# One kernel for attention and two expert layers: other forms of the routing comparisons beside layer two's products, ScalarE as the gate of four weight transfers, and another instruction order

## The chip, the cores and the metric

The program runs on one core of a Trainium2 chip. The metric is the device time of one execution in microseconds (us); the median of three runs counts. In the profile PE is TensorE, DVE is VectorE, ACT is ScalarE, POOL is GpSimd and SP is the queue that issues most transfers.

## What is computed

Attention over 4 x 8 heads (768 positions, head size 64, a few global keys and a local window), then an expert layer with a gate (layer one), then a second expert layer with a limit per expert (layer two). Of the reference, layer two matters here:

```python
cap = N // E                                   # 3072 // 8 = 384
logits = x @ w_gate
order = np.argsort(-logits.flatten())
for idx in order:
    tok, e = idx // E, idx % E
    if assigned[tok] >= 0 or counts[e] >= cap: continue
    assigned[tok] = e; counts[e] += 1
for e in range(E):
    h = np.maximum(x[assigned == e] @ w1[e], 0.0)
    out[assigned == e] = h @ w2[e]
```

## The kernel before, in words

**Layer two's products.** Each of the eight experts gets exactly 384 tokens. An expert's work is a *unit*: eight blocks `f`, each with 12 products into `ph` (384 columns; the inputs are split in a high and a low float32r part, so `xh,wh`, `xl,wh` and `xh,wl`) and 9 products into three banks `py` (512 columns). That is 168 products for a unit and 1344 for the layer.

**Routing (`phase`, `slots`, L1738 and L1859).** The greedy assignment is done in eight phases. In a phase each free token holds its best logit (`m`) and its expert (`oh`, one-hot). The phase finds the highest threshold at which some expert has more than its remaining places, fills that expert and takes it out. The threshold is found by seven comparisons (`BITS`: six of five bits with 32 thresholds each, and a last one of two bits with 4). One comparison is: VectorE compares all tokens with the thresholds (`gm`), TensorE counts per expert (`pr<-oh,gm`), VectorE picks the next threshold. A count comes in two forms:

- *direct*: 24 small products of 32 rows by 8 columns, one for each group of 128 tokens, then VectorE's flags `fl`, one more product with the table `wt`, and a VectorE maximum;
- *grouped* (`CG = 4`): 6 products of four token groups each, of which only a quarter of the result is wanted, a copy `cs` on VectorE, and a product that adds the quarters up. From phase 2 on (`LEAN`) the copy masks and one product with `sel` is enough (*lean*); otherwise there are four with `sels`. VectorE then takes the maximum, a 32 x 32 transpose and a weighted sum, with no flag product.

In the kernel before, the first 13 comparisons of all (`DIRECT`) are direct: phase 0 whole and six of phase 1. A phase's last comparison, of 4 thresholds, is always followed by the flag product, and from phase 1 on it is grouped in a narrow form (16 columns, four products with `identh`). After the comparisons a phase adds a visit with two products `pr<-c,tri`, a visit with `pr<-part,ones`, and two in `slots` (`pt<-ttb`, `pt<-tb_rhs,mp`), whose result is the expert's list of tokens, `ids`. GpSimd then gathers the expert's rows (`xg<-x2d,ids`, three transfers), TensorE transposes them (`x_turn`), ScalarE writes `xh` and VectorE `xl`.

**What sets the order.** Phase 0 runs beside the last second-layer products of layer one (`py`, 417 to 450 us), phase 1 begins before the first unit and goes on beside it, and phase p runs beside unit p - 1. All instructions are recorded through a planner: `Clock` holds a time for each engine with a cost for every operation (`cost`), and before each product `hook` (L1240) asks every open *stream* (routing, row lists, transpositions) whether its next step would be ready (`when`, L1223); if so, the step is recorded there, so TensorE's queue gets it ahead of the product. TensorE works in that order and waits when a step's operand is late. While nothing else is to be done `warm` fills TensorE with `ph<-ones,tri`.

**Weights.** A chunk of 512 KB comes into one of four buffers `wr`; ScalarE writes its high part `wh`, GpSimd (in four pieces) or VectorE the low part `wl`. Around the start of layer two, four transfers are held back by a 1 x 1 write into their buffer (`do_load`, `gate`), which the transfer has to follow: by VectorE before the change. The loop at the kernel's end (L2023) lets them go one by one as the first unit's blocks are turned.

Nearly all instructions carry L132, the recording helper's line, so rows are told apart by their tiles.

Of the kernel before, what the change touches and what calls it, by code (L numbers as in the profile page):

```python
# [19 lines left out]
class Clock:  # L20
# [4 lines left out]
    def __init__(self):  # L25
        self.at = dict.fromkeys(("pe", "dve", "act", "pool", "sp", "dma"), 0.0)
        self.seen, self.slots, self.count, self.log = {}, {}, {}, {}
        self.on = False
        self.late, self.fine = 0, False
# [46 lines left out]
    def cost(self, eng, op, outs, ins, extra):  # L76
        n = max([1] + [a.free_size() for a in outs[:1] + ins])
        if eng == "pe":
# [6 lines left out]
            return max(0.027, n * (2 if op == "transpose" else 4 if d.endswith("float32") else 1) / 2400.0)  # L85
# [85 lines left out]
def tile_attn_moe_moe(ctx: ExitStack, tc: tile.TileContext, q, k, v, n_global, n_local,  # L171
# [277 lines left out]
    class Weights:  # L449
# [58 lines left out]
        def do_load(self, i):  # L508
# [4 lines left out]
            if self.gate:  # L513
                nc.vector.memset(t[0:1, 0:1], 0.0)
# [46 lines left out]
    LATE = 0.3  # L561
# [649 lines left out]
    class Stream:  # L1211
# [287 lines left out]
    tabs = [rt.tile([128, 32], I32, name="tabf")] + [rt.tile([128, n_], I32, name=f"tab{s_}") for s_, n_ in BITS[1:]]  # L1499
    wt_ = rt.tile([32, 128], BF, name="wt")  # L1500
# [33 lines left out]

    blocks = identh.rearrange("p (j n) -> p j n", n=32)
# [22 lines left out]
    def ww_rest():  # L1558
# [4 lines left out]
                + [rt_rows, rt_sel, rt_sels])  # L1563
# [167 lines left out]
    def phase(ph_):  # L1731
# [8 lines left out]
        for it, (s_, n_) in enumerate(() if last else BITS):  # L1740
            if it and any(s_.kind == 'x' for s_ in streams):
                yield "dve", ()
            gm_ = rt.tile([128, NT * 32], BF, name="gm")
            gm = gm_[:, :NT * n_].rearrange("p (t n) -> p t n", n=n_)
# [44 lines left out]
            if wide:  # L1789
                df = rt.tile([128, E], F32, name="df")  # L1790
                fr = rt.tile([128, 2, 32], F32, name="fr")
                dv.tensor_tensor_reduce(df, cnt[:, :E], rem, 1.0, -3.0e38, op0=OP.subtract, op1=OP.max,
                                        accum_out=v_[:, 0:1])
                dv.transpose(fr[:, 0], v_[:, 0:1].to_broadcast([128, 32]))
                dv.scalar_tensor_tensor(fr[:, 1], fr[:, 0], 0.0, wrow_p, op0=OP.is_ge, op1=OP.mult, accum_out=v_[:, 1:2])
# [14 lines left out]
            else:  # L1810
                dv.scalar_tensor_tensor(nx[:, 1, :nn], val.to_broadcast([128, nn]), s_, nx[:, 0, :nn],
                                        op0=OP.logical_shift_left, op1=OP.bitwise_xor)
# [3 lines left out]
        if last:  # L1816
            dv.scalar_tensor_tensor(fo[:, 0], rem, 1e8, first, op0=OP.is_lt, op1=OP.mult)
        else:
            dv.scalar_tensor_tensor(fo[:, 0], pn_, v_[:, 1:2], first, op0=OP.is_equal, op1=OP.mult)
        dv.tensor_reduce(fx[:, 0:1], fo[:, 0], axis=AX.X, op=OP.max)  # L1820
        wait_for(lambda: not [s_ for s_ in streams if s_.kind == "ids"])
        yield "dve", ()
        fe = rt.tile([128, 6, NT], F32, name="fe", bufs=2)
        if not last:
            ts_ = thr.bitcast(F32)
            sc, g1 = fe[:, 2:4], fe[:, 1]
# [16 lines left out]
        if last:  # L1843
            yield "dve", ()
            dv.tensor_scalar(fe_p, PEN, 0.0, None, op0=OP.is_ge)
            dv.scalar_tensor_tensor(fe[:, 4], AC, fx[:, 0:1], fe_p, op0=OP.is_equal, op1=OP.add)
# [12 lines left out]
        dv.tensor_tensor(fe[:, 4], fe_p, g1, op=OP.add)  # L1859
        start("ids", slots(ph_, fe, fx))  # L1860
        yield "dve", ()
        go = rt.tile([128, NT, E], BF, name="go")
        part = rt.tile([128, E], BF, name="part")
        dv.tensor_tensor(go, oh, bc_e(gt[:, 0]), op=OP.mult)
        dv.tensor_tensor(gt[:, 0], gt[:, 0], g1, op=OP.add)
        with nc.allow_low_precision(reason="whole numbers up to 24"):
# [199 lines left out]
```

## Time and profile before

| what | value |
|---|---|
| median of three runs (lowest to highest) | 775.62 us (775.53 to 776.88) |
| the profiled execution's own time | 777.47 us |
| its span, first to last instruction | 775.7 us |
| PE busy | 744.8 us, 96% |
| DVE, ACT, POOL busy | 526.1, 403.3, 468.2 us |
| layer two: first product to last | 464.57 to 770.40 us |
| before it, filler, routing and the first gather | 450.52 to 464.57 us |

The page's own second section shows PE at nine tenths or more in 20 of 40 slices and PEclk at nine tenths or more in all. A busy PE is not one at its peak: busy time counts a product from start to modelled end, and products overlap. So the rows below are read by the distance from one start to the next.

### The profile page before, as it was taken

How to read it: one execution, taken by the hardware profiler on the slowest of the kernel's cores; microseconds unless marked ns; L12 is line 12 of the kernel's file. 1: busy time of each engine (PE TensorE's matmuls, PEld its weight loads, DVE VectorE, ACT ScalarE, POOL GpSimd, SP SyncE). 2: the span in 40 equal slices, each digit the busy share in tenths (PEclk: the TensorE clock that was granted, in tenths of full speed). 3: DMA queues.
4: the chain of work that ended last, by engine and by line, in shares of the span. 5: the costliest groups of instructions: out<-in, count | busy, mean ns of one | idle time of the engine just before them, and what ended most of it. 6: DMA issues, size and time to landing. Idle time of an engine off the chain costs nothing.

```text
span 775.7 us, 17432 instructions
## 1 busy us (share of the span) xinstructions
PE 744.8 (96%) x5910; PEld 628.7 (81%) x5910; DVE 526.1 (68%) x1952; ACT 403.3 (52%) x936; POOL 468.2 (60%) x821
## 2 busy tenths in 40 slices
PE   7999999899889999999999999999999999999997
PEld 5887777677659999999888677878788878788986
DVE  5987988979556676777634586778787778752110
ACT  5887787887547655555652113434333434255221
POOL 4664456755214464555793636975768777689911
PEclk9999999999999999999999999999999999999999
DMA  8686988897716766777760035626262636366311
GB/s 192 167 213 167 248 232 200 222 231 199 236 27 213 265 198 195 252 234 224 210 220 33 19 91 191 209 91 222 77 204 84 230 108 206 125 195 185 121 41 41
DMA packets 145370, 132.23 MB, mean 170 GB/s; under 512 B 65427, under 2 KB 112787, under 8 KB 145280
## 3 DMA queue, kind: packets, MB, share of 16 engines
q1 hardware_dynamic: 136896, 111.19, 48.9%
q0 software_dynamic: 6784, 19.51, 7.4%
q8 instruction: 48, 0.79, 0.4%
q10 hardware_dynamic: 1600, 0.39, 0.2%
q14 instruction: 42, 0.34, 0.1%
HBM read 108.80 MB, written 22.79 MB: 170 GB/s over the span
## 4 chain that ended last, share of the span: by engine, by line
PE 44%; POOL 8%; issue 6%; DMA 5%; DVE 4%; ACT 3%; POOLq 0%; DVEq 0%; ACTq 0%; SPq 0%
PE py L132 19%; PE ph L132 19%; POOL wl L132 7%; DMA wr<-in_moe_w_dram 4%; PE pr L132 3%; PE pt L132 3%; ACT wh L132 2%; DVE wl L132 1%; POOL out_dram L132 1%; DMA xg<-x2d,ids 1%; DVE py L132 1%; ACT ya L132 0%; DVE h L132 0%; POOL xg L132 0%; DVE o L132 0%
## 5 line engine op out<-in xcount | busy, mean ns | idle before, releaser
L132 POOL TENSOR_TENSOR wl<-wr,wh 128x256 fp32r<-128x256 f32 x356 | 253.6, 745 | 62.0 <-ACT wh L132 61.3
L132 ACT ACTIVATE wh<-wr 128x1024 fp32r<-128x1024 f32 (+1 forms) x148 | 142.2, 985 | 42.8 <-DMA wr<-in_moe_w_dram 26.8
L132 PE MATMUL py<-wh,h 128*128 128x512 f32 (+1 forms) x448 | 155.9, 401 | 0.0
L132 ACT ACTIVATE h<-ph 128x208 fp32r<-128x208 f32 (+2 forms) x132 | 54.4, 415 | 180.7 <-PE ph L132 168.3
L132 POOL TENSOR_SCALAR pb<-pb,st 128x232 f32<-128x232 f32 (+1 forms) x192 | 83.4, 453 | 74.3 <-ACT pb L132 24.2
L132 ACT ACTIVATE pb<-sb,st 128x232 f32<-128x232 f32 (+1 forms) x192 | 113.8, 664 | 10.1 <-DVE st L132 9.8
L132 DVE SCALAR_TENSOR_TENSOR h<-ph,h 128x208 fp32r<-128x208 f32 (+1 forms) x128 | 58.8, 460 | 88.8 <-ACT h L132 88.7
L132 PE MATMUL ph<-xh,wh 128*128 128x208 f32 (+1 forms) x512 | 99.1, 310 | 1.4 <-DVE h L132 1.4
L132 PE MATMUL ph<-xh,wl 128*128 128x208 f32 (+1 forms) x512 | 100.0, 311 | 0.0
L132 PE MATMUL ph<-xl,wh 128*128 128x208 f32 (+1 forms) x512 | 99.0, 311 | 0.0
L132 PEld LDWEIGHTS py<-wh,h 128*128 128x128 f32 (+1 forms) x448 | 82.0, 185 | 14.1
L132 PE MATMUL py<-wl,h 128*128 128x512 f32 (+1 forms) x224 | 90.9, 406 | 0.0
L132 PEld LDWEIGHTS ph<-xh,wh 128*128 128x128 f32 x512 | 82.2, 190 | 6.8 <-DVE h L132 1.6
L132 PEld LDWEIGHTS ph<-xl,wh 128*128 128x128 f32 x512 | 78.9, 190 | 1.1 <-issue 1.0
L132 PEld LDWEIGHTS ph<-xh,wl 128*128 128x128 f32 x512 | 78.9, 190 | 0.5 <-issue 0.3
L132 DVE TENSOR_TENSOR wl<-wr,wh 128x1024 fp32r<-128x1024 f32 x47 | 61.0, 1304 | 15.3 <-ACT wh L132 15.2
L132 DVE CUSTOM_DVE_ANT_0 sb<-pS,bias 128x232 f32<-128x232 f32 (+1 forms) x192 | 61.4, 374 | 8.9 <-PE pS L132 7.6
L132 DVE COPY pts<-pP 116x512 f32<-116x512 f32 (+1 forms) x96 | 60.7, 672 | 7.6 <-PE pP L132 7.1
L132 POOL DMA_INDIRECT xg<-x2d,ids x24 | 23.8, 990 | 52.2 <-DVE ids L132 19.1
L132 PE MATMUL pS<-kt,qt 64*128 64x232 f32 (+1 forms) x384 | 50.7, 382 | 1.0 <-ACT pb L132 1.0
L132 PE MATMUL pP<-ident,pb 128*116 128x128 f32 (+1 forms) x384 | 51.3, 277 | 0.0
L132 PE MATMUL pO<-pts,vw 116*64 116x128 f32 x640 | 46.3, 281 | 4.0 <-DVE pts L132 3.2
(465 smaller groups left out, 1267.5 us busy)
## 6 DMA issues: line engine op xcount, KB each, us to landing
wr<-in_moe_w_dram SPq DMA_DIRECT2D x136, 512.0 KB
xd<-xs SPq DMA_DIRECT2D x32, 192.0 KB
x2d<-xs SPq DMA_DIRECT2D x32, 192.0 KB
kraw<-in_k_dram SPq DMA_DIRECT2D x30, 192.0 KB
qraw<-in_q_dram SPq DMA_DIRECT2D x30, 192.0 KB
vw<-in_v_dram SPq DMA_DIRECT2D x32, 160.0 KB
vw<-in_v_dram SPq DMA_DIRECT2D x32, 120.0 KB
xT<-in_moe_w_dram SPq DMA_DIRECT2D x1, 1536.0 KB
```

Source lines behind the costliest of these rows:

```text
L132: r = f(*a, **k)
```

## The change

The change leaves what is computed as it is. Direct counts are used only until layer two's first unit has begun (`unit_no < 0`), in place of the first 13. From phase 2 on the last comparison has 32 thresholds like the others (`lean_low`), with two tables of their own (`tab8`, `zero8`, made once by `rt_eights`; and `jrow`), and takes the lean grouped form without flag product. Also from phase 2 on, `part` is computed early (`above`), and its product stands in one visit with the two of `tri`. The gate's 1 x 1 writes are ScalarE's, and a gate opens when a block is turned (`len(xt)`), not when its low part is recorded. The planner's costs for layer two are raised: 0.016 us for each float32r product, 0.085 us for a long product behind a short one. `LATE` goes from 0.3 to 0, and two kinds of waiting (`gm`, `ids`) get rules of their own in `when`. Renumbered planes of `fe` are left out of the diff here.

```diff
@@ Clock.cost
-            return max(0.027, n * (2 if op == "transpose" else 4 if d.endswith("float32") else 1) / 2400.0)
+            t = (0.016 if self.fine and d.endswith('float32r') else 0) + max(0.027, n * (2 if op == "transpose" else 4 if d.endswith("float32") else 1) / 2400.0)
+            back, self.short = self.short and t > 0.1, t < 0.06
+            return t + (0.085 if back else 0)
@@ Weights.do_load
-                nc.vector.memset(t[0:1, 0:1], 0.0)
+                nc.scalar.activation(t[0:1, 0:1], pcol[0:1], AF.Copy)
-    LATE = 0.3
+    LATE = 0.0
@@ Stream.when
+            if eng == "gm":
+                return ck.at["dve"] - 0.1
+            if eng == "ids":
+                return 1e9 if [s_ for s_ in streams if s_.kind == "ids"] else ck.at["dve"] - T_SP
@@ phase
             if it and any(s_.kind == 'x' for s_ in streams):
-                yield "dve", ()
+                yield "gm", ()
+            low = it + 1 == len(BITS)
+            lean_low = low and ph_ >= LEAN
+            n_ = 32 if lean_low else n_
-            nn = BITS[it + 1][1] if it + 1 < len(BITS) else 1
+            nn = 1 if low else 32 if ph_ >= LEAN else BITS[it + 1][1]
-            tb_ = tabs[it + 1] if it + 1 < len(BITS) else zero
+            tb_ = zero8 if lean_low else zero if low else tab8 if ph_ >= LEAN and it + 2 == len(BITS) else tabs[it + 1]
-            low = it + 1 == len(BITS)
-            direct = ph_ * len(BITS) + it < DIRECT
-            wide = not direct and not low
+            direct = unit_no[0] < 0
+            wide = not direct and (not low or lean_low)
...
-                dv.tensor_tensor_reduce(df, cnt[:, :E], rem, 1.0, -3.0e38, op0=OP.subtract, op1=OP.max,
-                                        accum_out=v_[:, 0:1])
+                if lean_low:
+                    dv.tensor_tensor(df, cnt[:, :E], rem, op=OP.is_ge)
+                    dv.tensor_tensor_reduce(df, df, first, 1.0, 0.0, op0=OP.mult, op1=OP.max, accum_out=v_[:, 0:1])
+                else:
+                    dv.tensor_tensor_reduce(df, cnt[:, :E], rem, 1.0, -3.0e38, op0=OP.subtract, op1=OP.max,
+                                            accum_out=v_[:, 0:1])
...
-        wait_for(lambda: not [s_ for s_ in streams if s_.kind == "ids"])
-        yield "dve", ()
+        yield "ids", ()
...
+        both = ph_ > 1
+        if both:
+            above()
-        yield "pe", [c2]
+        yield "pe", [c2, part] if both else [c2]
         te(pp[:, 0, 0:1], tri2, c2[:, 0:1], start=True, stop=False)
         te(pp[:, 0, 0:1], tri, c2[:, 1:2], start=False, stop=True)
+        if both:
+            pq = pp[:, 1, :E]
+            te(pq, ones, part, start=True, stop=True)
...
@@ end of the kernel
-        wait_for(lambda: units2[0].tb == tb, True)
+        wait_for(lambda: len(units2[0].xt) >= tb, True)
```

How the order moves is shown at three places. The first is VectorE just before layer two's first product, in phase 1's first two comparisons (`xl` is the low part of one turned block; the `gm` of two pieces is one comparison's). Before:

```order
L132 TENSOR_TENSOR gm<-m,py_7060 128x512
L132 TENSOR_TENSOR gm<-m,py_7060 128x256
L132 TENSOR_TENSOR py_7060<-tab_4447,py_7060 128x32
L132 TENSOR_TENSOR xl<-pt,xh 128x4x128
L132 MEMSET wr 1x1
L132 TENSOR_TENSOR xl<-py_7748,xh 128x4x128
L132 MEMSET wr 1x1 x3
L132 TENSOR_TENSOR fl<-pr,rem 32x8
L132 TENSOR_TENSOR xl<-py_7784,xh 128x4x128
```

and now:

```order
L134 TENSOR_TENSOR fl<-pr,rem 32x8
L134 TENSOR_TENSOR xl<-pt,xh 128x4x128
L134 TENSOR_REDUCE v__7725<-pr 128x1
L134 TENSOR_SCALAR py_7064<-v__7725 128x1
L134 TENSOR_SCALAR vi<-v__7725 128x1
L134 TENSOR_TENSOR py_7064<-tab_4446,py_7064 128x32
L134 TENSOR_TENSOR py_7064<-py_7064,vi 128x32
L134 TENSOR_TENSOR xl<-py_7733,xh 128x4x128
L134 TENSOR_TENSOR gm<-m,py_7064 128x512
L134 TENSOR_TENSOR gm<-m,py_7064 128x256
L134 TENSOR_TENSOR py_7064<-tab_4447,py_7064 128x32
L134 TENSOR_TENSOR xl<-py_7763,xh 128x4x128
```

The low parts of the first and second block now stand ahead of the second comparison's `gm`, and the four 1 x 1 writes are gone.

The second is TensorE in phase 2, from the fourth comparison's product with `sel` to the start of the next count. Before:

```order
L132 LDWEIGHTS sel
L132 MATMUL pr<-cs,sel 128x32
L132 MATMUL py_7894<-wl,h_8414 128x512
L132 MATMUL py_7894<-wh,h_8414 128x512
L132 MATMUL ph<-xh,wh 128x384 x4
L132 MATMUL ph<-xl,wh 128x384 x4
L132 MATMUL ph<-xh,wl 128x384 x4
L132 LDWEIGHTS gm
L132 MATMUL pr<-oh,gm 128x32
```

and now:

```order
L134 MATMUL pr<-cs,sel 128x32
L134 MATMUL py_7899<-wh,h_8372 128x512
L134 MATMUL py_7899<-wl,h_8372 128x512
L134 MATMUL py_7899<-wh,h_8372 128x512
L134 MATMUL py_7900<-wh,h_8372 128x512
L134 MATMUL py_7900<-wl,h_8372 128x512
L134 MATMUL py_7900<-wh,h_8372 128x512
L134 MATMUL py_7901<-wh,h_8372 128x512
L134 MATMUL py_7901<-wl,h_8372 128x512
L134 MATMUL py_7901<-wh,h_8372 128x512
L134 MATMUL ph<-xh,wh 128x384
L134 LDWEIGHTS gm
```

Between the two stood two products of 512 columns and twelve of 384; now nine of 512 and one of 384 stand there.

The third is GpSimd, from one of the last gathers to the gather for the last unit (`out_dram` is an expert's result being written). Before:

```order
L132 DMA xg_10968<-x2d,ids 128x512
L132 DMA xg_10970<-x2d,ids 128x512
L132 DMA xg_10972<-x2d,ids 128x512
L132 TENSOR_TENSOR wl<-wr,wh 128x256 x32
L132 DMA xg_11259<-x2d,ids 128x512
L132 DMA xg_11261<-x2d,ids 128x512
L132 DMA xg_11263<-x2d,ids 128x512
L132 TENSOR_TENSOR wl<-wr,wh 128x256 x8
L132 MEMSET spacer 1x1
L132 DMA out_dram<-o_11253,ids 3072x512
```

and now:

```order
L134 TENSOR_TENSOR wl<-wr,wh 128x256 x8
L134 MEMSET spacer 1x1
L134 DMA out_dram<-o_10879,ids 3072x512
L134 TENSOR_TENSOR wl<-wr,wh 128x256 x8
L134 MEMSET spacer 1x1
L134 DMA out_dram<-o_10881,ids 3072x512
L134 TENSOR_TENSOR wl<-wr,wh 128x256 x4
L134 MEMSET spacer 1x1
L134 DMA out_dram<-o_10883,ids 3072x512
L134 TENSOR_TENSOR wl<-wr,wh 128x256 x12
L134 DMA xg_11207<-x2d,ids 128x512
L134 DMA xg_11209<-x2d,ids 128x512
```

The last unit's gather (the second one of the two) stood behind 32 pieces of `wl` in a row. Now there are 32 pieces between the two gathers as well, but three results are written among them.

## Rows read from the trace of the kernel before

**Rows 1.** Stages: start:end, length, busy (x) of PE, PEld, DVE, ACT, POOL, clock, DMA.
```profile
464.57:770.40 305.83, 304.02 (x1853) 256.12 (x1851) 187.66 (x761) 118.17 (x171) 215.21 (x312) 1.00 0.45 146
```

**Rows 2.** Groups by form, layer two, PE: direct counts, narrow last counts | busy, mean ns.
```profile
L132 PE MATMUL pr<-oh,gm 128*32 128x8 bf16 x96 | 3.0, 167 | 0.5 <-DVE gm L132 0.5
...
L132 PE MATMUL pr<-oh,gm 128*16 128x32 bf16 x36 | 1.8, 177 | 0.0
```

**Rows 3.** Timeline of PE, unbroken products: start, us, operation, xcount.
```profile
531.26 0.85 PE L132 MATMUL ph<-xl,wh 128*128 128x384 f32 x4
...
532.65 0.40 PE L132 MATMUL py<-wh,h 128*128 128x512 f32 x1
...
552.51 0.40 PE L132 MATMUL py<-wh,h 128*128 128x512 f32 x1
...
554.57 0.33 PE L132 MATMUL ph<-xh,wh 128*128 128x384 f32 x1
```

**Rows 4.** Timeline of PE, phase 1: one direct comparison.
```profile
466.38 0.51 PE L132 MATMUL ph<-xh,wl 128*128 128x384 f32 x2
466.82 0.76 PE L132 MATMUL pr<-oh,gm 128*32 128x8 bf16 x24
467.51 0.62 PE L132 MATMUL ph<-xh,wl 128*128 128x384 f32 x2
...
468.97 0.85 PE L132 MATMUL ph<-xl,wh 128*128 128x384 f32 x4
```

**Rows 5.** Timeline of PE, phase 2: one lean comparison, and the next count.
```profile
509.79 0.39 PE L132 MATMUL py<-wl,h 128*128 128x512 f32 x1
510.02 0.32 PE L132 MATMUL pr<-oh,gm 128*128 128x32 bf16 x6
...
510.75 0.19 PE L132 MATMUL pr<-cs,sel 128*128 128x32 f16 x1
...
511.11 0.39 PE L132 MATMUL py<-wh,h 128*128 128x512 f32 x1
...
513.43 0.32 PE L132 MATMUL pr<-oh,gm 128*128 128x32 bf16 x6
```

**Rows 6.** Timeline of PE, phase 2: first and last row around a last comparison.
```profile
518.79 0.62 PE L132 MATMUL py<-wh,h 128*128 128x512 f32 x2
...
521.51 0.86 PE L132 MATMUL ph<-xh,wh 128*128 128x384 f32 x4
```

**Rows 7.** Timeline of PE, phase 2: the visit with part.
```profile
526.88 0.18 PE L132 MATMUL pr<-part,ones 128*128 128x8 bf16 x1
...
527.52 0.86 PE L132 MATMUL ph<-xh,wl 128*128 128x384 f32 x4
```

**Rows 8.** Timeline of PE at layer two's start.
```profile
459.59 0.76 PE L132 MATMUL pr<-oh,gm 128*32 128x8 bf16 x24 [0.29 <-DVE gm L132]
...
463.23 0.66 PE L132 MATMUL py<-ident,xg 128*128 128x128 f32 x4
...
464.57 0.62 PE L132 MATMUL ph<-xh,wh 128*128 128x384 f32 x2
```

**Rows 9.** Timeline of ACT at layer two's start.
```profile
463.92 0.60 ACT L132 ACTIVATE xh<-py 128x512 fp32r<-128x512 f32 x1 [0.99 <-PE py L132]
```

**Rows 10.** Timeline of DVE: the fifth gm of phase 2, and a block's low part.
```profile
512.13 0.95 DVE L132 TENSOR_TENSOR gm<-m,py 128x768 bf16<-128x768 f32 x1
...
516.59 0.55 DVE L132 SCALAR_TENSOR_TENSOR h<-ph,h 128x384 fp32r<-128x384 f32 x1
```

**Rows 11.** Timeline of PE, unit 0: a wait [idle before <-releaser].
```profile
471.23 0.76 PE L132 MATMUL pr<-oh,gm 128*32 128x8 bf16 x24 [0.48 <-DVE gm L132]
```

**Rows 12.** Timeline of PE, unit 0: another wait.
```profile
497.94 0.63 PE L132 MATMUL pt<-ident,xg 128*128 128x128 f32 x4 [0.62 <-DMA xg<-x2d,ids]
```

**Rows 13.** Timeline of PE, unit 6: a third wait.
```profile
711.00 0.63 PE L132 MATMUL pt<-ident,xg 128*128 128x128 f32 x4 [0.70 <-DMA xg<-x2d,ids]
```

**Rows 14.** Timeline of POOL before that third wait.
```profile
684.35 22.28 POOL L132 TENSOR_TENSOR wl<-wr,wh 128x256 fp32r<-128x256 f32 x32
706.78 0.95 POOL L132 DMA_INDIRECT xg<-x2d,ids  x1 [0.15 <-issue]
```

More of the change, by code (lines that the diff above doesn't have):

```diff
@@ L28, in __init__ @@
         self.on = False
-        self.late, self.fine = 0, False
+        self.late, self.fine, self.short = 0, False, False
     def place(self, t):
@@ L1845, in phase @@
             dv.tensor_scalar(fe_p, PEN, 0.0, None, op0=OP.is_ge)
-            dv.scalar_tensor_tensor(fe[:, 4], AC, fx[:, 0:1], fe_p, op0=OP.is_equal, op1=OP.add)
+            dv.scalar_tensor_tensor(fe[:, 3], AC, fx[:, 0:1], fe_p, op0=OP.is_equal, op1=OP.add)
             start("ids", slots(ph_, fe, fx))
@@ L1852, in phase, with above @@
                                 accum_out=fx[:, 2:3])
-        yield "pe", [c2]
+        go = rt.tile([128, NT, E], BF, name="go")
+        part = rt.tile([128, E], BF, name="part")
+        def above():
+            dv.tensor_tensor(go, oh, bc_e(gt[:, 0]), op=OP.mult)
+            with nc.allow_low_precision(reason="whole numbers up to 24"):
+                dv.tensor_reduce(part, go.rearrange("p t e -> p e t"), axis=AX.X, op=OP.add)
+        both = ph_ > 1
+        if both:
+            above()
+        yield "pe", [c2, part] if both else [c2]
         pp = fps.tile([128, 2, 64], F32, name="pr")
@@ L1856, in phase @@
         te(pp[:, 0, 0:1], tri, c2[:, 1:2], start=False, stop=True)
+        if both:
+            pq = pp[:, 1, :E]
+            te(pq, ones, part, start=True, stop=True)
         dv.tensor_tensor(fx[:, 1:2], fx[:, 2:3], pp[:, 0, 0:1], op=OP.subtract)
         dv.scalar_tensor_tensor(g1, sc[:, 1], fx[:, 1:2], gq[:, 1], op0=OP.is_le, op1=OP.mult)
-        dv.tensor_tensor(fe[:, 4], fe_p, g1, op=OP.add)
+        dv.tensor_tensor(fe[:, 3], fe_p, g1, op=OP.add)
         start("ids", slots(ph_, fe, fx))
         yield "dve", ()
-        go = rt.tile([128, NT, E], BF, name="go")
-        part = rt.tile([128, E], BF, name="part")
-        dv.tensor_tensor(go, oh, bc_e(gt[:, 0]), op=OP.mult)
+        if not both:
+            above()
         dv.tensor_tensor(gt[:, 0], gt[:, 0], g1, op=OP.add)
-        with nc.allow_low_precision(reason="whole numbers up to 24"):
-            dv.tensor_reduce(part, go.rearrange("p t e -> p e t"), axis=AX.X, op=OP.add)
         dv.tensor_tensor(gt[:, 1], gt[:, 0], code, op=OP.mult)
@@ L1870, in phase @@
         dv.tensor_tensor(AC, AC, gt[:, 1], op=OP.add)
-        yield "pe", [part]
-        pq = fps.tile([128, 2, 64], F32, name="pr")
-        te(pq[:, 0, :E], ones, part, start=True, stop=True)
+        if not both:
+            yield "pe", [part]
+            pq = fps.tile([128, 2, 64], F32, name="pr")[:, 0, :E]
+            te(pq, ones, part, start=True, stop=True)
         dv.tensor_scalar(fo_p[:, 0], fo_p[:, 1], -2 * BIG, BIG, op0=OP.mult, op1=OP.add)
@@ L1876, in phase @@
         dv.tensor_tensor(ML, ML, bc_t(fo_p[:, 0]), op=OP.min)
-        dv.tensor_tensor(rem, rem, pq[:, 0, :E], op=OP.subtract)
+        dv.tensor_tensor(rem, rem, pq, op=OP.subtract)
         yield "dve", ()
@@ L1882, in slots @@
         ttb = rt.tile([128, 1], BF, name="ttb")
-        dv.tensor_tensor_scan(fs_p, fe[:, 4], wrow_p[:, :NT], 0.0, op0=OP.add, op1=OP.bypass)
+        dv.tensor_tensor_scan(fs_p, fe[:, 3], wrow_p[:, :NT], 0.0, op0=OP.add, op1=OP.bypass)
         dv.tensor_copy(ttb, fs_p[:, NT - 1:NT])
@@ L1937, in tile_attn_moe_moe @@
     fo_p = in_bank(2 * E).rearrange("p (a e) -> p a e", a=2)
+    jrow = in_bank(32)
+    nc.vector.tensor_scalar(jrow, jint, 2.0 ** 23, None, op0=OP.add)
     nc.vector.tensor_copy(tab0, tabs[0])
```

29 lines of the change are left out of this document (21 added, 8 removed).

## Prediction

> **What bounds the kernel now.** I read the stages first, then TensorE's timeline inside the longest stage that the change touches, then the waits there. [...] In unbroken stretches eight products of 384 columns take 1.39 us from start to start, 0.174 us each, and nine of 512 columns take 2.06 us, 0.229 us each [rows 3]. The layer has 768 of the first and 576 of the second: 133.6 + 131.9 = 265.5 us. The other 40 us of the stage are routing, transpositions, the slow restart of products behind them, and waits. The change works on these 40.
>
> **The price of a visit.** I take the distance between two products around a visit and subtract the products between. A direct comparison: 468.97 - 466.38 = 2.59 us, less eight products of 0.174, is 1.20 us; up to 467.51, where the 24 small products are done, 0.78 of it is spent, and the rest is the flag product and restarts [rows 4]. A lean comparison: 511.11 - 509.79 = 1.32 us, less four products of 0.229, is 0.40 us, of which the count has 0.27 (510.02 to 510.75, less two products) and the product with sel 0.13 [rows 5]. A phase's last comparison: 521.51 - 518.79 = 2.72 us, less seven products of 0.229, is 1.12 us [rows 6]. The visit with part: 527.52 - 526.88 = 0.64 us, less three of 0.174, is 0.12 us [rows 7].
>
> **The change part by part.** The sum is made against the profiled execution's own 777.47 us, which is 1.85 us above the median of the three runs; the gains are subtracted from either.
>
> *Last comparisons.* Phases 2 to 6 have one each. With 32 thresholds it is the same three instructions on TensorE as in [rows 5], so each goes from 1.12 to 0.40 us: 5 x 0.72 = 3.6 us less. VectorE has one small instruction more there. If TensorE waited 0.15 us for it each time, 2.85 us would be left.
>
> *Phase 1.* Four direct comparisons stand in layer two now (96 small products, 24 each [rows 2]), besides the flag product of a fifth, about 0.3 us. In the new order one direct comparison is left there, the second of the phase, and four are grouped with four sels products. That form is in no row: it lies between the lean product, 0.13, and a row of narrow products with their own restarts, some 0.37 if I divide a last comparison's 1.12 us evenly over its three visits. I take 0.22, since the four products are as full as the lean one, so a comparison is 0.27 + 0.22 = 0.49 us. Sum: 4 x 1.20 + 0.30 - 1.20 - 4 x 0.49 = 1.9 us less; with 0.13 it is 2.3, with 0.37 it is 1.3. The phase's narrow last comparison stays, one of the six in [rows 2].
>
> *part.* Five visits of 0.12 us become one more small product each in a visit that exists, about 0.03 us: 0.45 us less. Against that, seven transpositions share a visit with a sel product in the old order, five in the new: 2 x 0.09 = 0.2 us more.
>
> *The start of layer two.* The first product at 464.57 follows ScalarE's cast of the third block, 463.92 to 464.52 [rows 9], which follows its transposition at 463.23 [rows 8]. That transposition stood behind 16 products of the second comparison, which waited for VectorE. In the new order this comparison stands behind the first product, and the first block is turned 8 products earlier. From 459.59 [rows 8] I add what now stands ahead of the third cast: 24 small products 0.7 us [rows 4], three sets of transpositions of 0.66 us, 1.5 in all where the next product covers the tail [rows 8], and for a flag, eight fillers and restarts 1.4 us, an estimate. That gives 463.2 instead of 463.23 + 0.66 = 463.9 us: 0.7 us earlier. If the third block's rows arrive late it is nothing, at most 1.2. The four 1 x 1 writes leave VectorE, which had them just there, and go to ScalarE, which is idle 0.99 us before the cast [rows 9]; I cost them at nothing. Without that cover they would delay the cast, and with it the first product, by what they take. [...]
>
> *Waits.* Three long ones show: 0.48 us for a direct comparison's gm [rows 11], 0.62 us for unit 1's rows [rows 12], 0.70 us for the last unit's [rows 13]. The first goes with its comparison, but I expect it again, 0.5 us, at the direct comparison that is left: its gm now follows two low parts on VectorE. Of the second I keep half, since 36 pieces of wl instead of 32 precede that gather, though their first transfers are let go earlier. The third arose because GpSimd worked off 32 pieces from 684.35 to 706.63 and gathered at 706.78 [rows 14], 4.2 us before the transposition at 711.00. There the new order gathers once unit 5's list of pieces is done, and turns the first block 22 products after unit 6's start; by the same 22.3 us for 32 pieces and about 4 us for three results after the gather before, I put the rows there some 3 us ahead, an estimate, and let the wait go. Sum: 1.8 - 0.5 - 0.3 = 1.0 us less.
>
> *A tighter round.* From sel (510.75) to the end of the next gm (512.13 + 0.95 = 513.08) VectorE needs 2.33 us, and TensorE began the next count at 513.43, so there was 0.35 us to spare [rows 5, 10]. In the new order nine products of 512 columns and one of 384 fill this round: 2.24 + 0.13 = 2.37 us. The reserve is gone, and a block's low part of 0.55 us [rows 10] in the round would be waited for. I take 0.6 us in all, between nothing and the slower rival below.
>
> Sum: -3.6 - 1.9 - 0.45 + 0.2 - 0.7 - 1.0 + 0.6 = -6.85. From the median 775.62 that is 768.8 us (770.6 for an execution like the profiled one). Before 450 us only a few routing visits move by a product or two, beside products that set the pace; I cost that at nothing.
>
> **The rivals.** *VectorE becomes the bound (slower).* 39 grouped comparisons lie in layer two in the new order, most in rounds of 2.3 to 2.5 us. If a low part of 0.55 us falls into two rounds of three, each such round needs 2.9 us, and TensorE waits 0.4 us in 26 of them: 10.4 us more, 775.6 - 7.4 + 10.4 = 778.6 us. It decides from 0.19 us of wait for each comparison (7.4 / 39). For it: the reserve of 0.35 us is used up. Against it: the round needs only 2.33 us as it is, and low parts stood in old rounds too without a wait. [...] The lean round's whole chain of small instructions, 2.33 us, lay under TensorE's cover so far [rows 5, 10].
>
> *Gathers come late.* GpSimd's pieces are spread among more results, and unit 6's rows are turned sooner after their list than any before. Waits like 0.62 and 0.70 us [rows 12, 13], up to 1.2, at three units more: 2 to 3.6 us back, 771 to 772.5 us. For it: two such waits are there now. Against: GpSimd is busy 215 of 306 us [rows 1].
>
> *The gain is hidden.* If the comparisons only stretch the phases and a later list holds up a unit, fixed gains turn into waits, within 0.2% of 775.6 us. Against: in the new order the lists are found earlier in the units than before, not later.
>
> *Everything falls well.* No new wait, the start 1.2 us earlier, all old waits gone: 775.6 - 6.0 - 1.2 - 1.8 = 766.6 us.
>
> **How the numbers follow.** Forecast, 767.5 to 770.5 us: 0.60. Late gathers: 0.20. Everything well: 0.08. Hidden: 0.07. Slower: 0.05. The range 766.3 to 772.6 us takes in the first three. About 0.2% (1.55 us) is what a measurement tells from no change: faster 0.88, same 0.07, slower 0.05.
>
> **What would show it.** Right: 24 small products in layer two, not 96; no flag products from phase 2 on; the first product near 463.9 us; lean last comparisons at 0.40 us; a stage of about 300 us. Wrong: waits on gm or cs of over 0.1 us in most comparisons (VectorE), waits on xg at three or more units (gathers), or grouped comparisons of phase 1 well above 0.5 us.

## The result, and the profile after

The changed kernel takes 786.07 us (median of 5 runs, 785.44 to 786.29); the kernel before took 776.01 on the same chip. The ratio is 1.0127 with a 95% interval of 1.0113 to 1.0141. It is **slower by 10 us**, where 768.8 us was forecast.

The profile page of the changed kernel, span and busy times (the profiled execution took 786.29 us):

```profile
span 784.5 us, 17299 instructions
...
PE 744.2 (95%) x5829; PEld 626.6 (80%) x5829; DVE 536.4 (68%) x1992; ACT 404.7 (52%) x940; POOL 472.2 (60%) x825
```

Its stage from layer two's first product to the last, by windows (busy us of each engine, granted clock, DMA share, GB/s):

```profile
466.15:779.39 313.24, 304.31 (x1795) 254.48 (x1795) 197.75 (x800) 119.04 (x171) 218.42 (x316) 1.00 0.43 143
```

Against [rows 1] the stage is 7.41 us longer and TensorE's busy time is the same. It stands idle for 313.24 - 304.31 = 8.93 us there, before the change for 1.81. So the loss shows as idle time of TensorE, at an unchanged clock (1.00 in both). (The visits were to need some 6 us less, so a part of the waiting lies in the busy time too: ends of products are modelled, 0.40 us of busy time for one of 512 columns where 0.229 us lies between two starts [rows 3], and a wait shorter than a product's tail counts as busy; x4 below shows how much that can be.) The changed kernel's waits of PE in layer two (line waited for: us in total, times, longest) say for whom:

```profile
PE pr L134 <- DVE part L134: 4.8, 5, 1.3
PE pt L134 <- DVE mp L134: 2.1, 5, 0.6
PE pt L134 <- DVE ttb L134: 0.9, 2, 0.5
PE pt L134 <- DMA xg<-x2d,ids: 0.6, 1, 0.6
PE pr L134 <- DVE ei L134: 0.2, 1, 0.2
```

Before, three waits of [rows 11 to 13], 1.8 us, were all. Four of these five lines are VectorE. Here is PE's timeline in phase 2's last comparison, in its new form, and the joint visit of `c` and `part` (start, us, instruction, in brackets the idle time before):

```profile
517.79 0.52 PE L134 MATMUL ph<-xl,wh 128*128 128x384 f32 x2
518.25 0.32 PE L134 MATMUL pr<-oh,gm 128*128 128x32 bf16 x6
518.41 0.42 PE L134 MATMUL ph<-xl,wh 128*128 128x384 f32 x1
518.67 0.34 PE L134 MATMUL ph<-xh,wl 128*128 128x384 f32 x1
518.85 0.19 PE L134 MATMUL pr<-cs,sel 128*128 128x32 f16 x1
518.88 0.78 PE L134 MATMUL ph<-xh,wl 128*128 128x384 f32 x3
519.50 0.39 PE L134 MATMUL py<-wh,h 128*128 128x512 f32 x1
...
522.29 0.69 PE L134 MATMUL ph<-xl,wh 128*128 128x384 f32 x3
522.83 0.20 PE L134 MATMUL pr<-c,tri 128*128 128x1 bf16 x2
523.81 0.17 PE L134 MATMUL pr<-part,ones 128*128 128x8 bf16 x1 [0.78 <-DVE part L134]
523.83 0.42 PE L134 MATMUL ph<-xl,wh 128*128 128x384 f32 x1
```

The comparison costs 519.50 - 517.79 less seven products of 0.174 us, 0.49 us, against 1.12 in [rows 6]: the forecast saving is there. But three microseconds later, in the visit that was to save 0.09 us, TensorE waits 0.78 us for `part`. VectorE's timeline of the same phase:

```profile
520.69 0.54 DVE L134 TENSOR_SCALAR py<-m,py 128x24 f32<-128x24 f32 x2
521.26 0.53 DVE L134 SCALAR_TENSOR_TENSOR py<-code,fx,py 128x24 f32<-128x24 f32 x2
521.83 0.26 DVE L134 TENSOR_TENSOR_SCAN fe<-py,ML 128x48 f32<-128x48 f32 x1
522.12 0.16 DVE L134 TENSOR_REDUCE c<-fe 128x2 bf16<-128x2 f32 x1
...
522.88 0.35 DVE L134 TENSOR_TENSOR go<-oh,py 128x192 bf16<-128x192 bf16 x1
523.26 0.49 DVE L134 TENSOR_REDUCE part<-go 128x8 bf16<-128x192 bf16 x1
```

From the first of the four instructions at 520.69 to the next one, which needs their result, it is 1.14 us. The planner's formula gives each of the four 0.067 + 0.06 + 24/960 = 0.15 us, and 0.127 us (`gap`) between an instruction and one that needs its result: 0.74 in all. `go` and `part` take 0.87 us to 523.75; planned are 0.267 + 0.127 + 0.267 = 0.66. Over the whole stretch, from 520.69 to the end of `part`, it is 3.06 us where the same formulas give 2.26. The 0.80 us between them is the size of the wait. The old planner made the same mistakes, but it also took a product for 384/2400 = 0.160 and 512/2400 = 0.213 us, where [rows 3] have 0.174 and 0.229, and a restart behind a visit for nothing, where the visit of [rows 7] costs 0.12 us with its restart: over a unit 96 x 0.014 + 72 x 0.016 = 2.5 us, and more for the restarts, by which TensorE ran behind its own plan. The change puts these two TensorE costs right and leaves VectorE's.

### The profile page after: what moved, and what is told of

It is laid out like the page before. It is cut to its first block, busy times and chain, and to the rows that moved or that the text cites. A ratio compares the mean times of both kernels' runs of the same rounds, so it can differ in the third digit from the quotient of the medians.

```text
span 784.5 us, 17299 instructions
## 1 busy us (share of the span) xinstructions
PE 744.2 (95%) x5829; PEld 626.6 (80%) x5829; DVE 536.4 (68%) x1992; ACT 404.7 (52%) x940; POOL 472.2 (60%) x825
## 4 chain that ended last, share of the span: by engine, by line
PE 41%; DVE 10%; issue 7%; DMA 5%; POOL 5%; ACT 2%; POOLq 0%; SPq 0%; ACTq 0%; DVEq 0%
PE ph L134 18%; PE py L134 17%; DMA wr<-in_moe_w_dram 4%; POOL wl L134 3%; PE pr L134 3%; PE pt L134 3%; DVE py L134 3%; ACT wh L134 2%; DVE h L134 1%; POOL out_dram L134 1%; DVE wl L134 1%; DVE fe L134 1%; DMA xg<-x2d,ids 1%; ACT ya L134 0%; DVE fr L134 0%
## 5 line engine op out<-in xcount | busy, mean ns | idle before, releaser
L134 PE MATMUL py<-wh,h 128*128 128x512 f32 (+1 forms) x448 | 157.6, 404 | 0.0
L134 ACT ACTIVATE pb<-sb,st 128x232 f32<-128x232 f32 (+1 forms) x192 | 113.9, 665 | 10.1 <-DVE st L134 9.7
L134 PE MATMUL ph<-xl,wh 128*128 128x208 f32 (+1 forms) x512 | 101.2, 312 | 0.0
L134 PEld LDWEIGHTS py<-wl,h 128*128 128x128 f32 (+1 forms) x224 | 41.5, 185 | 7.7 <-issue 1.3
```

The costliest lines, as they stand in the source:

```text
L134: r = f(*a, **k)
```

## The experiments

In the tables, "stage" is layer two's first to last product (start to start), then the time of units 0 to 5 (first product to the next unit's), then the **lead** of units 1 to 6: from the start of VectorE's `ids<-pt,ix`, which writes a unit's list, to the unit's first product. The batches ran on different chips, on which the kernel before took 775.97 to 782.94 us by its medians, so runs are compared by their ratio to the kernel before in the same batch. For reference:

| kernel | stage | units 0 to 5 | lead of units 1 to 6 |
|---|---|---|---|
| before | 305.6 | 42.1 38.7 38.8 38.8 38.9 37.5 | 15 14 15 17 19 19 |
| changed | 312.8 | 41.0 41.1 40.9 42.1 41.0 36.0 | 14 18 23 30 34 34 |

### First batch: what makes TensorE wait?

**x1**, the changed kernel with the old TensorE costs:

```diff
-            t = (0.016 if self.fine and d.endswith('float32r') else 0) + max(0.027, ...
+            t = max(0.027, ...
-            return t + (0.085 if back else 0)
+            return t
```

> The changed kernel, with the two terms that the change adds to the planner's cost of a TensorE instruction (0.016 us per product, 0.085 us behind a small one) taken out again. Theory A (reserve): in the kernel before, the planner counted TensorE's layer-two queue some 11% too short and VectorE's small instructions some 0.09 us too short each; the first error hid the second, and the change mends only the first, so that products of the routing stand too early and TensorE waits for VectorE. Then this run loses most of the 12 us of extra waits, the joint visit of c and part costs 0.1 to 0.3 us instead of 1.23, layer one is as before, and the time is 768 to 773 us. Theory B (joint visit): the two long instructions on go and part ahead of the visit are the cause by themselves; then the visit still costs about 1 us and the time is 779 to 783 us. Theory C (VectorE is too full for grouped comparisons): 783 us or more, in any order.

**x2**, the changed kernel with VectorE's costs put right too:

```diff
-            return 0.067 + 0.06 * extra + n / ...
+            return (0.157 if self.fine else 0.067) + 0.06 * extra + n / ...
-        return (0.0 if to == "pe" else 0.127) if frm == to else self.FAR[frm]
+        late = 0.09 if self.fine and frm == "dve" else 0.0
+        return (0.0 if to == "pe" else 0.127 - late) if frm == to else self.FAR[frm] - late
```

> The changed kernel, with the planner's VectorE costs in layer two raised by the 0.09 us by which the rows of the changed kernel exceed them (0.16 us for a planned 0.07, 0.95 for 0.87, 0.25 for 0.15), and the gaps behind an instruction shortened by as much, so that a chain of dependent ones is planned as before and a row of independent ones longer. TensorE's new costs stay. Theory A: the waits for VectorE in layer two go from some 15 us to 3 to 5, first to last product 299 to 302 us instead of 312.8, time 773 to 776 us (the 2.3 us lost in layer one stay). Theory B: 780 to 784. Theory C: 784 or more.

**x3**, the changed kernel with `part` in a visit of its own:

```diff
-        both = ph_ > 1
+        both = False
```

> The changed kernel, with part multiplied in a visit of its own in every phase, as in the kernel before. Theory A: the five joint visits lose their 1.23 us, 6.1 in all, but the visits that follow are planned with the same costs and wait again, 0.2 to 0.5 us each: 781 to 784 us. Theory B: all of the joint visits' wait goes, 6 us, and with it half of the loss: 779 to 781 us. Theory C: within 1.5 us of 786.

**x4**, the kernel before with nothing but x1's two terms added.

> The kernel before, with nothing but the change's two new terms in the planner's cost of a TensorE instruction. Theory A: the reserve goes here too; waits for VectorE of 0.1 to 0.5 us at most visits of layer two, and layer one loses its 2 us: 781 to 786 us. Theory B: within 1.5 us of 776, since part has its own visit. Theory C: within 2 us of 776, since the comparisons are not changed.

| run | median us | ratio (95%) | stage | units 0 to 5 | lead of units 1 to 6 |
|---|---|---|---|---|---|
| x1 | 781.87 | 1.0103 (1.0047 to 1.0159) | 309.8 | 42.8 40.3 38.8 38.9 38.9 38.9 | 14 13 13 13 13 13 |
| x2 | 792.67 | 1.0220 (1.0196 to 1.0245) | 322.3 | 42.6 45.0 43.3 38.7 40.7 39.1 | 12 14 13 12 15 15 |
| x3 | 789.41 | 1.0176 (1.0152 to 1.0200) | 316.2 | 40.8 41.2 40.8 45.1 41.8 36.0 | 14 19 24 32 36 34 |
| x4 | 785.06 | 1.0116 (1.0099 to 1.0133) | 314.7 | 43.4 41.6 41.9 42.0 40.8 34.9 | 17 24 30 36 44 45 |

x4 fits theory A: two terms in a table of costs lose as much as the whole change. Few of its waits show as idle time. Its stage is 9.1 us longer than before, its idle time only 2.7 us (4.55 against 1.81). The rest is hidden behind modelled ends of products, as in this visit, which starts 0.55 us after a product that needs 0.229 us and counts 0.15 us as a wait (first the stage by windows):

```profile
463.02:777.76 314.74, 310.19 (x1852) 257.21 (x1851) 186.21 (x760) 117.99 (x171) 217.38 (x316) 1.00 0.44 142
```

```profile
551.65 0.40 PE L134 MATMUL py<-wh,h 128*128 128x512 f32 x1
552.20 0.19 PE L134 MATMUL pr<-c,tri 128*128 128x1 bf16 x2 [0.15 <-DVE ei L134]
```

From the start of a product to the start of a visit right behind it, less the product's 0.174 or 0.229 us, it is 14.6 us in all in x4's stage and 5.9 us in that of the kernel before. Which of the two terms does it was not tried. But x1 and x2 contradict it: taking the terms out, or putting VectorE's costs right, should have brought 768 to 776 us and did not. B falls with x3: without the joint visit the other visits wait instead (its one large wait is told of at the end). The leads showed what was missing. Where the order is tight (x3, x4, the change), lists come ever earlier and visits wait; where it is roomy (x1, x2), the lead sticks at 12 to 15 us and some units start late (in x1 units 1 and 6). That became theory D: a phase is one chain through both engines, about as long as a unit, and it can be paid for at either end.

### Second batch: each part of the change alone, in the old order

**x5** is x1 with x3's edit. **x6** is the kernel before with the change's `lean_low` lines (and the tables for it), **x7** with one line, **x8** with the change's `above` and `both` lines.

```diff
 x6
+            low = it + 1 == len(BITS)
+            lean_low = low and ph_ >= LEAN
+            n_ = 32 if lean_low else n_
...
 x7
-            direct = ph_ * len(BITS) + it < DIRECT
+            direct = unit_no[0] < 0
 x8
-        yield "pe", [c2]
+        yield "pe", [c2, part] if both else [c2]
...
```

> The changed kernel, with the planner's TensorE costs of before and with part in a visit of its own. Theory D (one chain): a phase of the routing is one chain that alternates between TensorE and VectorE and takes 36 to 39 us, about as long as a unit; what stands too early for VectorE is paid as a wait at the visit, and what stretches the phase is paid as a late list at the next unit's start. The joint visit puts two VectorE instructions, 0.35 and 0.49 us, into that chain in each phase. Then this run wins back the 3.9 us of joint visits of the run with old TensorE costs and 1 to 2 us of its late starts: 775 to 778 us. Theory E (the grouped comparisons and the new rules for when VectorE's steps are taken cost the rest): 780 to 783 us, as without part alone.

> The kernel before, with nothing but the last comparison of phases 2 to 6 in the common form (and the three small tables that it needs). By the prediction's sum 5 x 0.72 = 3.6 us less: 772 to 773 us. Theory D agrees if VectorE's part of the last comparison is no longer than that of the three narrow visits: 772 to 774. Theory E: the common form's longer VectorE part holds up the phase's end: 776 to 778.

> The kernel before, with nothing but the direct form ending at layer two's first unit instead of after thirteen comparisons. By the prediction's sum 1.9 us less: 773.5 to 774.5 us. Theory D: VectorE's part of a grouped comparison is longer than that of a direct one, so phase 1 ends 1 to 3 us later and unit 1's rows come late: 775 to 778. Theory E: 777 or more.

> The kernel before, with nothing but part multiplied in c's visit from phase 2 on. By the prediction's sum 0.45 us less: 775.5. Theory D: two VectorE instructions of 0.84 us together stand in the chain of five phases, planned as 0.53 us; the visits wait 0.3 to 0.8 us each in place of 0.11 and 0.09, and the lists come 0.9 us later in each phase: 777 to 781 us.

| run | median us | ratio (95%) | stage | units 0 to 5 | lead of units 1 to 6 |
|---|---|---|---|---|---|
| x5 | 791.05 | 1.0184 (1.0149 to 1.0219) | 318.7 | 42.9 40.3 39.2 38.8 40.2 44.4 | 14 14 14 13 13 17 |
| x6 | 784.03 | 1.0076 (1.0050 to 1.0101) | 311.4 | 42.1 38.9 41.9 41.3 38.3 37.5 | 15 14 16 15 15 14 |
| x7 | 782.60 | 1.0063 (1.0045 to 1.0080) | 310.4 | 43.2 41.7 39.0 38.9 39.1 37.3 | 14 15 17 19 21 21 |
| x8 | 783.74 | 1.0079 (1.0054 to 1.0103) | 312.1 | 42.3 39.8 39.8 39.8 39.7 38.9 | 15 15 14 14 14 13 |

Each of the three parts, priced as a gain, loses 5 to 6 us alone by its ratio, and more than theory D expected of x6, x7 and x8. In x8 the phases take what the units take, 39.7 us, with the lead going down to 13, and TensorE waits for rows at six places, 5.1 us in all. That fits a chain lengthened by the 0.84 us of `go` and `part`, which the units have to follow. x5 missed by 13 us; x13 in the third batch shows the same late starts, but why x1, which differs from x5 by the joint visit alone, is spared most of them stays open. In x6 one unit's start shows how such a loss is paid, first on PE's timeline, then by windows:

```profile
586.34 0.18 PE L132 MATMUL pr<-cs,sel 128*128 128x32 f16 x1 [0.92 <-DVE cs L132]
586.37 0.63 PE L132 MATMUL pt<-ident,xg 128*128 128x128 f32 x4
588.30 1.65 PE L132 MATMUL ph<-xh,wh 128*128 128x384 f32 x4 [1.29 <-ACT xh L132]
```

```profile
580.00:586.37 6.37, 5.46 (x42) 4.54 (x40) 4.84 (x16) 4.48 (x6) 6.21 (x10) 1.00 0.55 209
586.37:588.30 1.93, 0.64 (x6) 0.40 (x5) 1.57 (x8) 1.59 (x3) 1.93 (x4) 0.86 0.62 237
588.30:595.00 6.70, 6.70 (x25) 5.62 (x25) 4.02 (x14) 1.06 (x2) 4.46 (x7) 0.53 0.01 2
```

Unit 3's last block is turned at 586.37, its cast waits behind a weight's cast on ScalarE, and TensorE idles twice, 0.92 and 1.29 us. Then the granted clock is 0.53 for 6.70 us, and four products of `ph` take 1.65 us at 588.30, where those at 596.15, at a clock of 1.00 again, take 0.86: another 6.70 x 0.47 = 3.1 us, an estimate from this length and clock. This start alone, 0.92 + 1.29 + 3.1 = 5.3 us, is nearly all of the 5.8 us by which x6's stage is longer than before. x7 pays in the same way at unit 1's start: waits of 0.94, 1.14, 0.42 and 0.69 us from 505.41 us on, and a clock of 0.80, 0.50 and 0.85 in the three windows of 2 us from 508 us on. In x6 a late start thus cost its waits, 2.2 us, and by that estimate more than that again. It also means that x6 and x7 each lost through one place of one order.

### Third and fourth batch: roomy only where the lists have a lead

The flag `slow` is set from a unit on; where it is set, **x9** (from unit 2) and **x10** (from unit 1) use x2's VectorE costs. **x11** is x9 with x3's edit. **x12** uses the old TensorE costs where `slow` is set, with x3's edit.

```diff
             unit_no[0] = u
+            ck.slow = ck.fine and u >= 2
 x12
-            t = (0.016 if self.fine and d...
+            t = (0.016 if self.fine and not self.slow and d...
-            return t + (0.085 if back else 0)
+            return t + (0.085 if back and not self.slow else 0)
```

> The changed kernel, with the VectorE costs of the run 'vector costs' (0.09 us more an instruction, chains as before), but from layer two's unit 2 on alone; units 0 and 1 are planned as tightly as in the change. Theory D (one chain): a list must stand some 13 us ahead of its unit; in the changed kernel it is 9, 14, 18, 23, 30 and 34 us ahead, since the tight plan makes short phases and pays with 2 to 3 us of waits for VectorE in each unit; where the lead is there, a roomier plan costs nothing. Then units 2 to 4, 40.9, 42.1 and 41.0 us in the changed kernel, come down to 37.6 to 38.5 each, phases grow to 37 to 39 us, the lead stays over 13, and the time is 774 to 778 us. If VectorE itself cannot do a phase's work beside a unit's (theory C), the units stay at 40 us or more and the time at 783 or more.

> The same from unit 1 on. Theory D: unit 1's list stands 14 us ahead of its unit, hardly more than the 13 that it needs, so that the roomier phase 2 uses the lead up: late rows at units 2 and 3, 1 to 3 us each, and a time between the run from unit 2 on and the run with these costs all through layer two (792.7): 778 to 786 us. Theory C: 783 or more, and no different from the run from unit 2 on.

> The changed kernel with these VectorE costs from unit 2 on, and part in a visit of its own. Theory D: go and part, 0.84 us, leave the chain of each phase, at 0.09 us more on TensorE a phase: within 1.5 us of the run with the joint visit, better by up to 1 us if a list is still late there. Theory B (the joint visit costs by itself): 3 us better than that run.

> The changed kernel with the planner's TensorE costs of before from unit 2 on, tight ones until then, and part in a visit of its own. Theory D: with the lead of 18 us at unit 2 the roomy plan costs no late list until unit 5 or so: units of 37.6 to 38.5 us, 774 to 778 us, against 791.1 with the old costs all through. Theory C: 783 or more.

**x13** is x12 with `u >= 1`, **x14** is x12 without x3's edit, **x15** is x12 with x7's line taken back.

> As the run with the old TensorE costs from unit 2 on and part alone, but with the old costs from unit 1 on. Theory D: unit 1 takes 38.7 us, as in the kernel before, instead of 41.3, but the lead at unit 2 is 14 to 15 us instead of 19, close to the 13 that a unit needs; if it holds, 2 us less than that run (ratio to the kernel before 0.997); if it is used up, late rows at units 2 to 5 as in the run with the old costs all through (ratio 1.018), at least 1.005. Rival G (the old costs win because they are left longest): the more units are planned by the old costs the better, 0.997 without condition.

> As the run with the old TensorE costs from unit 2 on, but with part in c's visit, as in the change. Theory D: the two long instructions are in the chain again, planned 0.3 us too short together, so phases 3 to 6 take some 0.8 us more and the joint visit waits 0.5 to 0.8 us each in five units: 2 to 4 us slower than with part alone, ratio 1.002 to 1.005. The prediction's sum: 0.45 us faster than with part alone, ratio 0.999.

> As the run with the old TensorE costs from unit 2 on and part alone, but phase 1 keeps its direct comparisons, as in the kernel before. The prediction's sum: 1.9 us slower, ratio 1.002. Theory D: VectorE's chain of a direct comparison is shorter by the step on cs, so phase 1 ends no later and the lead at unit 1 stays; TensorE pays 1.9 us for it: 1.002 to 1.004. If phase 1's grouped form is what delays unit 1 (as in the kernel before with nothing but that), then 0.997.

| run | median us | ratio (95%) | stage | units 0 to 5 | lead of units 1 to 6 |
|---|---|---|---|---|---|
| x9 | 786.28 | 1.0077 (1.0050 to 1.0105) | 310.8 | 40.8 41.5 38.2 38.5 39.6 37.6 | 14 18 21 20 22 20 |
| x10 | 789.94 | 1.0122 (1.0088 to 1.0155) | 313.6 | 41.2 38.8 39.8 40.3 39.4 42.7 | 15 15 14 15 15 17 |
| x11 | 787.16 | 1.0092 (1.0066 to 1.0118) | 311.6 | 41.1 40.9 38.4 39.5 40.5 37.8 | 15 19 22 23 24 22 |
| x12 | 779.89 | 0.9997 (0.9981 to 1.0013) | 305.8 | 40.9 41.3 38.5 38.5 38.4 36.9 | 14 19 20 20 20 19 |
| x13 | 790.81 | 1.0177 (1.0139 to 1.0214) | 316.2 | 41.2 38.6 38.7 40.3 40.2 44.4 | 15 14 13 13 13 17 |
| x14 | 778.42 | 1.0013 (0.9995 to 1.0032) | 305.0 | 41.0 41.0 38.3 38.3 38.2 36.7 | 14 18 19 19 19 18 |
| x15 | 782.37 | 1.0051 (1.0026 to 1.0076) | 308.5 | 44.0 41.4 38.4 38.4 38.4 36.4 | 17 23 25 25 25 23 |

x12 and x13 differ in when one cost switches, one unit earlier, and are 1.8% apart. Unit 4's list and first product, x12's two rows and then x13's, give leads of 20.4 and 12.6 us:

```profile
606.50 0.16 DVE L134 SCALAR_TENSOR_TENSOR ids<-pt,ix 128x3 int32<-128x3 f32 x1
...
626.86 0.69 PE L134 MATMUL ph<-xh,wh 128*128 128x384 f32 x3
```

```profile
611.74 0.16 DVE L134 SCALAR_TENSOR_TENSOR ids<-pt,ix 128x3 int32<-128x3 f32 x1
...
624.38 0.79 PE L134 MATMUL ph<-xh,wh 128*128 128x384 f32 x3
```

With a lead the roomy order costs nothing, and units 2 to 4 take 38.2 to 38.5 us. Without, x13's units are slow from unit 3 on: units 3 to 5 (leads of 13) wait 0.6 us for a `gm` and 0.5 us for `xl` just behind their start, and unit 6 is the worst, with waits of 1.75, 1.21 and 0.69 us in a row and a clock of 0.54 for 5.36 us behind them. The first of these is for `mp` of the last unit's list, a visit that stands ahead of unit 6's last block in TensorE's order. (The lead is counted to the actual start, so a late start lengthens it: hence the 17 there.)

```profile
705.83 0.24 PE L134 MATMUL pt<-tb_rhs,mp 128*128 128x27 bf16 x3 [1.75 <-DVE mp L134]
707.28 1.09 PE L134 MATMUL pt<-ident,xg 128*128 128x128 f32 x4 [1.21 <-issue]
709.06 1.65 PE L134 MATMUL ph<-xh,wh 128*128 128x384 f32 x4 [0.69 <-ACT xh L134]
```

Rival G (the longer the old costs, the better) falls, and so does theory C: VectorE does a phase beside a unit of 38.3 us. x9 confirms D in units 2 and 3 only; it missed 774 to 778, since rows came late for units 5 and 7 (one wait of 2.55 us, then a clock of 0.50 from 714 to 716 us and 0.78 from 716 to 718), although the lists had 20 us and more. Why VectorE's true costs order those gathers worse than the old TensorE costs stays open. x11, x9 with `part` alone, is no better (1.0092), as D expected and B did not. x10, with leads of 14 and 15 us, loses more than x9, as D expected, and more than D's range. x14 contradicts D's price for the joint visit: where the lead is there it costs nothing (305.0 against 305.8 us). x14 is also the plainest test of the cause: the changed kernel with the old TensorE costs from unit 2 on, and the stage is 305.0 us in place of 312.8. The change's other edits (`LATE`, the rules for `gm` and `ids`, the gate) are all in x14 and were not tried alone.

### Last batch: between the two

**x16** switches in the middle of unit 1 (from its fifth step), **x17** lowers the term in steps; both are x14 otherwise.

```diff
 x16
+            ck.slow = ck.fine and s >= 12
 x17
-            t = (0.016 if self.fine and d...
+            t = (self.more if self.fine and d...
+            ck.more = (0.016, 0.008, 0.0)[min(u, 2)] if ck.fine else 0.016
-            return t + (0.085 if back else 0)
+            return t + (0.085 if back and self.more > 0 else 0)
```

> The changed kernel with the planner's TensorE costs of before from the middle of unit 1 on (its fifth step), joint visit kept. Theory D: half of the waits of unit 1 go (41.0 us to some 39.8), and the lead at unit 2 is 16 to 17 us, still over 13: 1 us less than with the switch at unit 2, ratio to the kernel before 0.998 to 1.000. If 16 us is already too little, the units from 2 on take 39 to 40 us and the ratio is over 1.006.

> The changed kernel with the added TensorE cost per product 0.016 us in unit 0, 0.008 in unit 1 and none from unit 2 on, joint visit kept. Theory D: as the run before, phase 2 neither as tight nor as roomy: unit 1 at 39 to 40 us, lead at unit 2 of 16 to 17 us, ratio 0.998 to 1.000; over 1.006 if that lead is too little.

| run | median us | ratio (95%) | stage | units 0 to 5 | lead of units 1 to 6 |
|---|---|---|---|---|---|
| x16 | 783.16 | 1.0000 (0.9983 to 1.0016) | 306.4 | 41.2 40.3 38.7 38.7 38.7 37.2 | 15 17 18 18 19 18 |
| x17 | 781.93 | 0.9979 (0.9962 to 0.9995) | 304.4 | 40.8 40.0 39.2 38.3 38.2 36.7 | 14 17 19 20 19 18 |

x17 is the only version measured ahead of both kernels: 0.2% faster than the one before, 1.5% faster than the changed one by their ratios. The margin over the kernel before is small (interval 0.9962 to 0.9995), and x17 is the best of seventeen versions, so part of it may be chance.

## Why the prediction was wrong

**The step that failed first** is that the sum counts each microsecond taken out of TensorE's queue as a microsecond of the time. A queue that is busy to 99% (304.02 of 305.83 us [rows 1]) can still be paced by a chain beside it. In the kernel before, lists stood 14 to 15 us ahead of units 1 to 3; x5 and x13 show late starts at 13, x1 at two units with 14 and 13, x6 one at 16. The shortest lead of any run is 12 us (x2); that a unit can't start much sooner behind its list is read from this and was not tried by itself. A phase took 37 to 39 us and a unit 38.8. x6, x7 and x8 took work out of that queue and lost 5 to 6 us. (By the page of the kernel before, PE is at nine tenths or more in 35 of 40 slices, not 20: the queue is still fuller than the section on the time before has it.)

**The second is the sum's term on a tighter round**, "I take 0.6 us in all". It measures some 7 us (idle time 8.93 against 1.81 us), and x4 and x14 show what makes it: the two raised planner costs alone lengthen the old kernel's stage by 9.1 us, and taking them back from unit 2 on shortens the changed kernel's by 7.8. The sum has no term for these costs, though they set the order. I had weighed the round of gm and cs, where VectorE had 0.35 us to spare, and not the phase's end, where no row of before showed a wait, as I read it because TensorE ran behind its plan. The old waits shrank from 1.8 to 0.6 us, where 0.8 was forecast; that is lost in this.

**The rivals.** *VectorE becomes the bound* had the sign and the engine; its place was wrong. No low part was at fault, and the rounds wait little: the waits are at `part`, `mp` and `ttb`, once a phase. That is 7.8 us in the first three lines of the waits, not 0.4 us in two rounds of three. The phase's end is a row of small instructions: in the changed kernel's layer two one that writes 2 elements takes 0.16 us (`c<-fe`), and those on 24 take from 0.17 (`AC<-AC,py`) to 0.25 us (`py<-m,py`) on the mean. *Gathers come late* is not what the changed kernel shows (0.6 us), but a unit's late start, by late rows or by their late turning, is the other half of the mechanism, in x1, x2, x5 to x8 and x13. *The gain is hidden* is not what the changed kernel shows either, since its lists are 14 to 34 us early; in x6 and x7 late rows and lists did not hide a gain but made a loss. *Everything falls well* has nothing for it.

**What held.** Grouped comparisons in phase 1: x15 against x12, 2.7 us of stage (by ratio 0.5%, 4 us) where 1.9 was the term. Joint visit: x14 against x12, 0.8 us of stage, not separated by ratio, where 0.45 was. Last comparisons: 0.49 us against 0.40 forecast; units 2 to 4 take 38.2 to 38.5 us where before took 38.8, so 0.3 to 0.6 of the 0.8 us per unit that the sum gave. The start: from the first deferred `py` to layer two's first product 46.55 us (419.60 to 466.15) against 47.27 (417.30 to 464.57), the 0.7 us forecast. From the first list to the first product it is 9.27 us against 9.93, in x1 9.49; but in x1 the list comes 0.4 us later, and its start gains nothing as a whole (47.25 us). The four 1 x 1 writes cost nothing, as forecast: ScalarE needs 0.18 us for the first and 0.37 us for the three others, and the cast behind them still waits 0.33 us for TensorE. The savings of the visits were thus there in good part and bought nothing, since the order that came with them had no reserve.

"Before 450 us ... nothing" is not refuted. The changed kernel's profile is 2.3 us later at 417 us, but x2 and x3, whose products come in the same order up to the first deferred `py` and which ran on one chip, reach that one at 416.9 and 418.4 us. In the code the 0.085 us is not limited to layer two, as the section on the change says (`fine` guards the 0.016 alone), so it can move products ahead of it too. A loss by that does not show: x1 without the term reaches the first deferred `py` at 417.7 us, x4 with it at 416.1, on the same chip. What of the 10 us lies ahead of layer two (10.1 by the medians, 7.3 by the stage) stays open.

## What to carry to other kernels

Before a visit is taken out of a full queue, measure the lead of what the queue will need next: the distance from a result to its first use, unit by unit. Where a static order comes from a table of costs, two errors in it may hold each other up. Here one side put right lost 1.2% (x4, in the kernel before) and both put right lost 2.2% (x2, in the changed one), so a truer table is no gain by itself: look whether the order that comes of it is too tight (waits at the visits) or too roomy (late starts). If both hurt, be tight until the lead is there and roomy afterwards; that brought the loss back with the old TensorE costs (x12, x14, x16, x17), and only in part with VectorE's (x9, x11).

## What was not expected of the hardware

In x6 the granted clock fell to 0.53 for 6.70 us behind two waits of TensorE that came close together at a unit's start (0.92 and 1.29 us), while in the changed kernel single waits of up to 1.27 us left it at 1.00. The length of a wait alone does not tell: for the last unit's rows TensorE waited 2.55 us in x9 and 2.66 us in x11, and the clock went to 0.50 in x9 (714 to 716 us) and stayed at 1.00 in x11.

In x3 one VectorE instruction on 8 elements took 2.78 us, where the same one takes 0.17 to 0.83 us in its five cases in the changed kernel and others of its form 0.17 there (522.79 is such a one). VectorE's row, then the windows:

```profile
588.27 2.78 DVE L134 CUSTOM_DVE_ANT_0 df<-df,first 128x8 f32<-128x8 f32 x1
```

```profile
588.00:593.70 5.70, 2.44 (x14) 2.01 (x13) 5.28 (x18) 0.49 (x1) 3.06 (x6) 0.95 0.00 1
593.70:595.00 1.30, 1.30 (x5) 1.11 (x6) 1.06 (x8) 0.41 (x1) 0.00 (x0) 0.50 0.00 0
595.00:598.00 3.00, 3.00 (x13) 2.24 (x13) 2.83 (x15) 1.38 (x3) 1.01 (x1) 0.73 0.74 257
```

TensorE waited 3.27 us for it and then had a clock of 0.50 and 0.73, 1.3 x 0.50 + 3.0 x 0.27 = 1.5 us more, an estimate from these windows; that accounts for unit 3's 45.1 us in x3's profiled execution; whether the others of that run had it too is not known. Hardly any transfer moved meanwhile (DMA share 0.00 from 588.00 to 595.00, against 0.43 from 463 to 790 us). What held the instruction was not tried.
